# An attention block and a gated feed-forward layer on one core: the quadratic table made from products of projected rows instead of squared pair differences, in a new order, with the activation table asked for at the start

## The chip, the core and the metric

The kernel runs on one core of a Trainium2 chip. The metric is the device time of one execution in microseconds (us), smaller is better. An execution is profiled by the hardware; the profile gives each instruction's start and duration on each engine: PE (matmuls; PEld is its weight load), DVE (VectorE), ACT (ScalarE), POOL (GpSimd) and SP (which only issues transfers here). PSUM is the memory that PE writes and DVE and ACT read; it has 8 banks of 512 floats on each of 128 partitions.

## What is computed

`x` holds 4 batches of 12480 rows of 128 numbers, `inducing` 32 rows. All is float32.

```python
def mab(q, kv):
    s = scale * (q @ kv.transpose(0, 2, 1))
    s = s - s.max(-1, keepdims=True)
    a = np.exp(s)
    a /= a.sum(-1, keepdims=True) + 1e-09
    return a @ kv
h = mab(I, x)
return mab(x, h).astype(np.float32)
...
h = x @ w_in
relu6 = np.clip(h + 3.0, 0.0, 6.0)
g = h * relu6 / 6.0
return (g @ w_out).astype(np.float32)
```

So each batch first gives 32 rows H (every inducing row attends over the whole batch), then each of the 49920 rows attends over its batch's 32 rows H, and the result goes through a feed-forward layer with 2048 hidden units (`w_in` 128x2048, `w_out` 2048x128).

## The kernel before, in words

A row's second attention output is a weighted mean of the 32 rows H with weights a. Its 2048 hidden values are the same mean of the 32 projected rows G = H @ w_in. Where these stay within 3 of zero, the activation is (g*g + 3g)/6, so the final output is linear in the weights (32 rows through the whole layer, the table `BD`) plus a quadratic part that depends on the weights only through products a_m * a_n. The square of a mean is the mean of the squares less the sum over pairs of a_m * a_n * (G_m - G_n)^2, so the quadratic part needs one row of 128 outputs for each of 512 pairs (m, m + k): the **quadratic table** `Cq`, 4 blocks of 128 pairs by 128 outputs, bf16, made once for each batch.

Each batch of 12480 rows is cut in six groups of 2048 rows (16 tiles of 128) and one of 192 rows (2 tiles of 96). For each batch b there are three kinds of work.

Phase 1, by half groups: load `xr` (`op_X`, a transfer that POOL issues), cast to bf16 (`op_K`, on DVE, ACT or POOL), transpose 8 tiles on PE (`op_T`), copy out of PSUM (`op_Y`), scores against the inducing rows (`op_S`), exponential on ACT (`op_E`), weighted sum of rows on PE (`op_A`), running sums on DVE or POOL (`op_H`, `op_D`). Five buffers `xr` hold the loaded groups, and eight `xT` the transposed ones, since phase 2 uses them again.

The tables of batch b: `op_c1` to `op_c6` end in `HT` (H transposed, L503). From it `op_c9` makes the scores' weights, `op_G`, `op_cH`, `op_L`, `op_cM`, `op_cN` the linear table `BD` (L589). For the quadratic one `op_cA` and `op_cB` (L523, L526) form 512 columns of pair differences `dH` on DVE; sixteen `op_M` (L532) project them, one 128x512 matmul for each block of 128 hidden units; sixteen `op_N` (L540) square them on ACT into the twelve buffers `sq`; sixteen `op_P` (L598), four 128x128 matmuls each, sum `sq` against `w_out` into one bank, and `op_cP` (L608) scales this into `Cq`.

Phase 2, by groups: scores (`op_Z`), exponentials on ACT (`op_Zd` into `dk`, `op_Ze` into `e`), `op_W`, four transfers that SP issues and that repeat `dk` over partitions into `d`, the sum of weights (`op_R`), its logarithm on ACT (`op_Rl`, L655), normalised exponent (`op_Rz`), `op_Ra` (ACT), `op_Rh`, the spread to pairs (`op_B`, PE), pair weights (`op_F`, L703, ACT, two banks at once, into `TF`), times `d` on DVE (`op_U`, L712, into `TD`), then PE sums over the pairs (`op_q`, L747, 8 matmuls of 128x128 for each call, `TF` and `TD` against `Cq`) and over the linear table (`op_l`, L729), and `op_v` (L758, DVE or ACT) copies the result out for `op_O`, a transfer that SP issues.

The order of everything is written out by hand: `ORDER` is one list of 1583 tokens, and each token calls one `op_` function: `N.0.5.2.A` is `op_N` of batch 0, hidden block 5, PSUM bank 2, on ACT. Each engine runs its own instructions in the order of the list; waits come from the data. Phase 1 of the next batch, the tables and phase 2 of the batch before are interleaved in it. The list also says on which engine a cast or a copy runs (`V` DVE, `A` ACT, `P` POOL) and which bank is used. ACT evaluates exponentials and logarithms from a loaded function table; the program holds an `ACT_TABLE_LOAD` wherever the loaded table lacks the next function. `op_it` asks for a table that holds both; in `ORDER` of before this token comes late, in batch 1's tables. `op_w` are matmuls on a zero tile at the start that compute nothing.

Of the kernel before, what the change touches and what calls it, by code (L numbers as in the profile page):

```python
# [9 lines left out]
FP32 = mybir.dt.float32  # L10
FP32R = mybir.dt.float32r
# [12 lines left out]
i0.- X.0.0.8.16 i1.- X.0.0.0.8 i2.- w.2.6 X.0.6.0.2 w.2.0 i4.5 K.0.6.0.2.A w.2.3 w.2.0 w.2.2 i3.V T.0.6.0.2.4 i8.- w.2.3  # L24
w.2.7 i5.5.V X.0.1.0.16 i9.P X.0.2.0.16 ia.- K.0.0.8.16.V Y.0.6.0.2.4.A X.0.3.0.16 S.0.6.0.2.0 E.0.6.0.2.0 w.2.2
K.0.1.8.16.A K.0.0.0.8.V K.0.1.0.8.V A.0.6.0.2.0 c2.0.- T.0.0.0.8.1 T.0.0.8.16.2 Y.0.0.0.8.1.V T.0.1.0.8.5 T.0.1.8.16.4
S.0.0.0.8.1 Y.0.1.0.8.5.V Y.0.0.8.16.2.A Y.0.1.8.16.4.A K.0.2.0.8.V wi.- S.0.0.8.16.1 X.0.4.0.16 S.0.1.0.8.5 T.0.2.0.8.7
K.0.2.8.16.V S.0.1.8.16.5 E.0.0.0.16.1 A.0.0.0.8.1 T.0.2.8.16.3 D.0.0.V Y.0.2.0.8.7.V K.0.3.8.16.V A.0.0.8.16.1
E.0.1.0.16.5 Y.0.2.8.16.3.A A.0.1.0.8.5 S.0.2.0.8.7 T.0.3.8.16.4 K.0.3.0.8.V S.0.2.8.16.7 D.0.1.V i6.P Y.0.3.8.16.4.V
i7.P A.0.1.8.16.5 E.0.2.0.16.7 T.0.3.0.8.2 H.0.0.1 wh.0.V H.0.1.5 wh.1.A A.0.2.0.8.7 Y.0.3.0.8.2.A wh.3.A wh.2.A  # L30
X.0.5.0.16 wl.1.V A.0.2.8.16.7 D.0.2.V K.0.4.0.8.V X.1.0.0.16 wo.- wl.2.V S.0.3.0.8.2 S.0.3.8.16.2 H.0.2.7 T.0.4.0.8.6
E.0.3.0.16.2 A.0.3.0.8.2 Y.0.4.0.8.6.A X.1.1.0.16 K.0.4.8.16.P K.0.5.8.16.P T.0.4.8.16.1 A.0.3.8.16.2 X.1.2.0.16
S.0.4.0.8.4 K.0.5.0.8.A D.0.3.V Y.0.4.8.16.1.V S.0.4.8.16.4 E.0.4.0.16.4 K.1.0.0.8.P T.0.5.0.8.5 wl.3.V T.0.5.8.16.1
# [24 lines left out]
H.1.4.1 E.1.5.0.16.2 B.0.3.0.2.0 W.0.3 D.1.5.V Zd.0.4.4 q.0.1.2.1.5 q.0.1.3.1.7 A.1.5.0.8.4 K.2.1.0.8.P F.0.3.0.0.2
l.0.1.3.7 l.0.2.3.2 l.0.1.2.5 c1.1.- l.0.2.2.3 U.0.2.1 F.0.3.0.1.0 S.1.6.0.2.1 E.1.6.0.2.1 v.0.1.2.5.V A.1.5.8.16.4
v.0.1.3.7.A q.0.2.3.0.2 A.1.6.0.2.5 T.2.0.0.8.7 Ze.0.4.6 Ra.0.3 H.1.5.4 X.2.3.0.16 H.1.6.5 U.0.3.0 c2.1.- q.0.2.3.1.2  # L60
v.0.2.3.2.V q.0.2.2.0.3 O.0.1.0.16 q.0.2.2.1.3 B.0.3.1.0.4 X.2.4.0.16 Y.2.0.0.8.7.A W.0.4 c3.1.7 K.2.2.0.8.P
T.2.0.8.16.2 v.0.2.2.3.A c4.1.7 q.0.3.1.0.3 c5.1.7 l.0.3.1.3 F.0.3.1.0.0 F.0.3.1.1.4 c6.1.7 R.0.4.1 c7.1.A Z.0.5.0.7
Z.0.6.4.5 Y.2.0.8.16.2.V K.2.2.8.16.P Rl.0.4.1 S.2.0.0.8.2 Ze.0.5.7 c8.1.P cB.1.V q.0.3.1.1.3 Zd.0.5.0 S.2.0.8.16.2
T.2.1.8.16.1 cA.1.V M.1.2.0 Zd.0.6.4 Ze.0.6.5 Rz.0.4.6 l.0.3.0.4 R.0.5.6 c9.1.P E.2.0.0.16.2 Y.2.1.8.16.1.A T.2.1.0.8.2
q.0.3.0.0.4 G.1.3.1 Rl.0.5.6 U.0.3.1 Rh.0.4.V Y.2.1.0.8.2.V G.1.2.1 O.0.2.0.16 K.2.3.8.16.P G.1.1.1 G.1.0.1 Ra.0.4
v.0.3.1.3.A N.1.2.0.A Rz.0.5.7 W.0.5 q.0.3.0.1.4 v.0.3.0.4.A B.0.4.0.2.6 F.0.4.0.0.2 q.0.3.3.0.0 l.0.3.3.0 F.0.4.0.1.6
Rh.0.5.V l.0.4.1.4 cH.1.1 q.0.3.3.1.0 M.1.3.2 cJ.1.1 l.0.3.2.3 cI.1.1 v.0.3.3.0.V R.0.6.1 q.0.3.2.0.3 Rl.0.6.1
q.0.3.2.1.3 U.0.4.0 N.1.3.2.A K.2.3.0.8.P B.0.4.1.6.0 Ra.0.5 q.0.4.1.0.4 L.1.0.2 q.0.4.1.1.4 Rz.0.6.5 v.0.3.2.3.V
D.2.0.P q.0.4.0.0.3 M.1.0.5 l.0.4.0.3 Rh.0.6.V v.0.4.1.4.V F.0.4.1.0.6 F.0.4.1.1.0 N.1.0.5.A O.0.3.0.16 U.0.4.1
# [100 lines left out]

TG = 16
RT = 4
NX = 5
NXB = 2
NXT = 8
NSQ = 12
NTF = 3
NTD = 2
NNF = 2
NE = 2  # L180
ND = 2
NOS = 2
# [13 lines left out]
def kernel(  # L196
# [8 lines left out]
    nc = tc.nc  # L205
# [774 lines left out]
```

## Time and profile before

| | |
|---|---|
| median of 3 runs | 308.41 us (304.93, 308.41, 309.09) |
| the profiled execution's own time | 310.61 us |
| its span, first to last instruction | 308.8 us |
| mean granted PE clock | 0.962 of full speed |
| bytes moved | 66.69 MB |
| `HT` of the four batches ready (L503) | 35.7, 91.1, 165.5, 231.6 us |
| `Cq` of the four batches ready (L608) | 58.4, 134.1, 200.6, 264.1 us |

How to read it: "busy" is the time in which an engine had an instruction under way. Matmuls are pipelined, so PE's busy time includes their overlap, and one matmul's mean duration (about 220 ns for 128 columns) is far above the distance at which they follow each other; that distance is read from the chain of waits, where runs of matmuls stand with their count. The chain of waits is followed back from the last instruction: at each step to what released it, or to the instruction ahead of it on its engine.

### The profile page before, as it was taken

What the parts mean: (1) busy time and instruction counts of PE and PEld (TensorE: products, weight loads), DVE (VectorE), ACT (ScalarE), POOL (GpSimd) and SP (SyncE); (2) the same over time, 40 slices, a digit from 0 to 9 for tenths busy, and PEclk for the clock granted to TensorE, in tenths of its full rate; (3) what the DMA queues carried; (4) which work ended last, traced back from release to release, by engine and by line L of the source; (5) the groups of instructions that cost most, each with busy time, mean ns of one, the idle gap of its engine ahead of it and who ended that gap; (6) DMA issues with size and microseconds to landing.
All of it is one profiled execution on the core that took longest, in us unless ns stands there. A gap on an engine that the chain in (4) does not pass through costs nothing.

```text
span 308.8 us, 9738 instructions
## 1 busy us (share of the span) xinstructions
PE 275.8 (89%) x4105; PEld 216.8 (70%) x4105; DVE 218.5 (71%) x386; ACT 255.7 (83%) x416; POOL 65.7 (21%) x101
## 2 busy tenths in 40 slices
PE   6797878978986788999969999999999999999990
PEld 1587657766775565888848777787777777777780
DVE  4299996756766465575975766989788783799861
ACT  1377989998889799888955999789889999999980
POOL 8225533120345001144414001042302000000000
PEclk9597999999999599999997999999999999999998
DMA  6999984438698035676997351657547733777944
GB/s 154 419 348 409 346 248 153 138 70 330 212 326 293 2 142 179 184 231 182 338 385 240 138 183 42 197 156 240 180 104 270 248 141 69 222 231 244 326 163 155
DMA packets 23312, 66.69 MB, mean 216 GB/s; under 512 B 3648, under 2 KB 16736, under 8 KB 16992
## 3 DMA queue, kind: packets, MB, share of 16 engines
q1 hardware_dynamic: 18928, 38.36, 38.4%
q0 software_dynamic: 4336, 27.66, 25.8%
q8 instruction: 33, 0.54, 0.7%
q14 instruction: 15, 0.12, 0.1%
HBM read 27.67 MB, written 25.56 MB: 172 GB/s over the span
## 4 chain that ended last, share of the span: by engine, by line
PE 64%; ACT 13%; DVE 9%; DMA 7%; issue 3%; SPq 1%; POOL 0%; ACTq 0%; DVEq 0%; POOLq 0%
PE ps L747 25%; PE ps L729 7%; PE ps L426 6%; PE ps L453 5%; DMA d<-dk 5%; PE ps L693 5%; PE ps L598 4%; PE ps L532 3%; ACT TF L703 3%; PE ps L621 3%; DMA xl<-in_x_dram 2%; PE ps L437 2%; ACT L655 2%; PE ps L650 2%; DVE TD L712 2%
## 5 line engine op out<-in xcount | busy, mean ns | idle before, releaser
L703 ACT ACTIVATE TF<-ps 128x1024 bf16<-128x1024 f32 (+1 forms) x100 | 96.2, 1005 | 8.8 <-PE ps L693 7.3
L712 DVE TENSOR_TENSOR TD<-TF,d 128x2048 bf16<-128x2048 bf16 (+1 forms) x52 | 61.1, 1177 | 13.3 <-ACT TF L703 11.7
L747 PE MATMUL ps<-Cq,TD 128*128 128x128 bf16 (+1 forms) x784 | 59.9, 222 | 0.1
L747 PE MATMUL ps<-Cq,TF 128*128 128x128 bf16 (+1 forms) x784 | 59.3, 221 | 0.2
L758 DVE COPY os<-ps 128x512 f32<-128x512 f32 x62 | 42.2, 688 | 22.8 <-PE ps L747 17.8
L747 PEld LDWEIGHTS <-TF 128*128 128x128 bf16 (+1 forms) x784 | 46.6, 99 | 11.2 <-issue 9.1
L747 PEld LDWEIGHTS <-TD 128*128 128x128 bf16 (+1 forms) x784 | 47.4, 100 | 6.9 <-issue 4.6
L729 PE MATMUL ps<-BD,a 128*128 128x512 f32 (+1 forms) x100 | 39.2, 463 | 0.0
L420 POOL CAST xb<-xr 128x1024 bf16<-128x1024 f32 x24 | 28.1, 1180 | 51.7 <-PE ps L426 39.1
L540 ACT ACTIVATE sq<-ps 128x512 bf16<-128x512 f32 x64 | 35.2, 617 | 1.5 <-PE ps L532 1.4
L453 PE MATMUL ps<-xr,a 128*32 128x128 f32 x384 | 31.8, 229 | 3.1 <-ACT ln L655 2.2
L426 PE MATMUL ps<-ident_b,xb 128*128 128x128 bf16 x384 | 30.8, 232 | 3.0 <-DVE xb L420 1.8
L432 DVE COPY xT<-ps 128x1024 bf16<-128x1024 bf16 x32 | 21.8, 687 | 13.0 <-PE ps L426 11.9
L453 PEld LDWEIGHTS ps<-xr,a 128*32 128x32 f32 x384 | 25.4, 111 | 5.6 <-ACT ln L655 3.0
L426 PEld LDWEIGHTS <-xb 128*128 128x128 bf16 x384 | 24.9, 105 | 6.1 <-issue 3.7
L693 PE MATMUL ps<-z,pair 32*128 32x256 f16 (+1 forms) x400 | 21.3, 272 | 7.9 <-ACT os L758 2.4
L416 POOL DMA_DIRECT2D xr<-in_x_dram x25 | 15.7, 630 | 49.5 <-PE ps L453 26.2
L532 PE MATMUL ps<-dH,w_hi 128*128 128x512 bf16 x64 | 22.2, 384 | 3.3 <-ACT dk L631 1.8
L758 ACT COPY os<-ps 128x512 f32<-128x512 f32 x34 | 19.7, 590 | 4.9 <-PE ps L747 2.7
L660 DVE CUSTOM_DVE_ANT_0 zz<-ln,ps 128x512 f32<-128x512 f32 (+1 forms) x28 | 17.3, 619 | 9.0 <-ACT ln L655 8.8
L729 PEld LDWEIGHTS ps<-BD,a 128*128 128x128 f32 (+1 forms) x100 | 18.3, 196 | 4.9 <-ACT dk L631 2.0
L432 ACT COPY xT<-ps 128x1024 bf16<-128x1024 bf16 x16 | 16.2, 1015 | 5.1 <-PE ps L426 5.1
(145 smaller groups left out, 415.5 us busy)
## 6 DMA issues: line engine op xcount, KB each, us to landing
out_dram<-os SPq DMA_DIRECT2D x24, 1024.0 KB, 4.8
xr<-in_x_dram POOLq DMA_DIRECT2D x23, 1024.0 KB, 7.6
d<-dk SPq DMA_DIRECT2D x96, 128.0 KB, 3.2
xr<-in_x_dram POOLq DMA_DIRECT2D x2, 512.0 KB, 5.5
os<-in_moe_w_in_dram POOLq DMA_DIRECT2D x1, 1024.0 KB, 13.5
w_or<-in_moe_w_out_dram POOLq DMA_DIRECT2D x1, 1024.0 KB, 8.7
xl<-in_x_dram POOLq DMA_DIRECT2D x4, 96.0 KB, 5.9
out_dram<-osl SPq DMA_DIRECT2D x4, 96.0 KB, 4.3
```

The source lines that it names most:

```text
L420: copier(e)(at(xb, xbl, b, g)[:p, lo:hi, :], at(xr, xl, b, g)[:p, lo:hi, :].bitcast(FP32))
L426: nc.tensor.transpose(pt[:, (i - lo) * p : (i - lo + 1) * p], at(xb, xbl, b, g)[:p, i, :], ident_b[:p, :p])
L432: copier(e)(xT_of(b, g)[:, lo * p : hi * p], ps[:, k, :].bitcast(BF16)[:, : (hi - lo) * p])
L453: nc.tensor.matmul(ps[:M, k, :C], lhsT=at(a1, a1l, b, g)[:p, i * M : (i + 1) * M], rhs=at(xr, xl, b, g)[:p, i, :], start=(i == 0), stop=(i ...
L532: nc.tensor.matmul(ps[:, k, :], lhsT=w_hi[:, jb, :], rhs=dH[:, :, :, :, :].rearrange("p q k m i -> p (q k m i)"),)
L540: nc.scalar.activation(sq_of(b, jb)[:, :], ps[:, k, :], ACT.Square)
L693: nc.tensor.matmul(ps[:, pairs[j // 2] + j % 2, f * w : (f + 1) * w], lhsT=pair[rows, f].rearrange("p m i -> p (m i)"), rhs=fat(z_, b, g)[ ...
L703: nc.scalar.activation(hat(TF_, b, g, h)[:, 2 * q : 2 * q + 2, :w], ps[:, k : k + 2, :w], ACT.Exp, scale=-1.0)
L712: nc.vector.tensor_mul(split(hat(TD_, b, g, h)), split(hat(TF_, b, g, h)), d.unsqueeze(2).to_broadcast([P, J, 2, w]),)
L729: nc.tensor.matmul(ps[:p, k, : J * C], lhsT=fat(a_, b, g)[:rows, s * p : (s + 1) * p], rhs=BD_[b % 2][:rows, :J, :].rearrange("p j c -> p ...
L747: nc.tensor.matmul(ps[:p, k, j * C : (j + 1) * C], lhsT=t[:, j, f * w + s2 * p : f * w + (s2 + 1) * p], rhs=Cq_[b % 2][:, (1 + f) if u els ...
L758: copier(e)(at(os_, osl, b, g)[:p, s * J : (s + 1) * J, :], ps[:p, k, : J * C].rearrange("p (j c) -> p j c", c=C),)
```

## The change

The pair differences, their projection and their squares go. For a pair, -(G_m - G_n)^2 / 2 is G_m * G_n - G_m^2 / 2 - G_n^2 / 2, so the kernel now projects the 32 rows once and multiplies projected rows. In order: `op_cU` (three small DVE instructions) takes the mean of the rows H off and scales; `op_cg`, sixteen matmuls of 32 columns, projects; `op_gx` copies the 16x32 results out of PSUM as bf16 with 16 columns repeated at the end (two instructions); `op_g1` makes a copy shifted by one column; `op_gq` squares (512 columns). Sixteen `op_m` a batch on DVE multiply a row block `near` (`gb`, or the shifted `g1`) with `gb` at four offsets, 512 products at a time, bf16, into the three buffers `pr`. `op_P` is one matmul with `w_out` as the stationary operand and 512 columns of products, where it was four of 128 columns; its result stands with outputs on the partitions. `op_cs` sums the squares against `w_out` (sixteen matmuls of 32 columns), `op_cS` scales them by -1/2, `op_cT` adds the two ends of each pair, `op_cW` adds this to the products' sum, `op_ct` transposes four blocks on PE and `op_cP` copies them into `Cq`.

`ORDER` is written anew, 1566 tokens. `op_it` is now the third token. The first loads are the two halves of group 0 and groups 1 to 3; the small last group follows. `op_w` calls go from 8 to 24 (16 to 48 matmuls). Casts `op_K` on ACT go from 4 to 19, on DVE from 22 to 9, on POOL from 26 to 24; copies `op_v` on ACT from 35 to 59, on DVE from 65 to 41. The rings `xl`, `xbl`, `a1l`, `osl` of the small last group go from two buffers to one.

```diff
-i0.- X.0.0.8.16 i1.- X.0.0.0.8 i2.- w.2.6 X.0.6.0.2 w.2.0 i4.5 K.0.6.0.2.A w.2.3 w.2.0 w.2.2 i3.V T.0.6.0.2.4 i8.- w.2.3
+X.0.0.0.8 i2.- it.- X.0.0.8.16 w.2.7 X.0.1.0.16 i0.- w.2.3 w.2.4 w.2.0 X.0.2.0.16 i1.- i4.4 i3.V w.2.5 w.2.1 K.0.0.0.8.A
...
-NSQ = 12
+NPR = 3
...
+    root = 1.0 / math.sqrt(3.0 * 1024.0)
...
-        sq_ = ring("sq", NSQ, [P, 512], BF16)
+        pr_ = ring("pr", NPR, [P, 4, 4, P], BF16)
+        gb = sb.tile([P, FB, M + 16], BF16, name="gb")
+        g1 = sb.tile([P, FB, M], BF16, name="g1")
+        gq = sb.tile([P, FB, M], BF16, name="gq")
...
-        def op_cA(b, e):
-            veng(e).tensor_sub(dH[:, 0], shifted(HT, 0, 1, 0), shifted(HT, 2, 0, 4))
-
-        def op_cB(b, e):
-            veng(e).tensor_sub(dH[:, 1], shifted(HT, 1, -1, 0), shifted(HT, 4, 0, 4))
...
-        def op_M(b, jb, k):
-            nc.tensor.matmul(
-                ps[:, k, :],
-                lhsT=w_hi[:, jb, :],
-                rhs=dH[:, :, :, :, :].rearrange("p q k m i -> p (q k m i)"),
-            )
-
-        def op_N(b, jb, k, e):
+        def op_cU(b, e):
+            nc.vector.tensor_reduce(hm[:, :], HT[:, 0, :], axis=AX.X, op=ALU.add)
+            nc.vector.tensor_scalar_mul(hm[:, :], hm[:, :], -root / M)
+            nc.vector.tensor_scalar(
+                hc[:, :], HT[:, 0, :], root, hm[:, 0:1], op0=ALU.mult, op1=ALU.add
+            )
+
+        def op_cg(b, k):
+            for jb in range(FB):
+                nc.tensor.matmul(ps[:, k, jb * M : (jb + 1) * M], lhsT=w_hi[:, jb, :], rhs=hc[:, :])
...
+        def op_gx(b, k, e):
+            copier(e)(gb[:, :, :M], g_of(k))
+            copier(e)(gb[:, :, M:], g_of(k)[:, :, :16])
+
+        def op_gq(b, e):
             if e == "A":
-                nc.scalar.activation(sq_of(b, jb)[:, :], ps[:, k, :], ACT.Square)
+                nc.scalar.activation(gq[:, :, :], gb[:, :, :M], ACT.Square)
...
+        def op_g1(b, e):
+            copier(e)(g1[:, :, :], gb[:, :, 1 : M + 1])
+
+        def op_m(b, q, f):
+            rows = slice(4 * q, 4 * q + 4)
+            one, off = ((0, 2), (1, 2), (1, 4), (0, 4))[f]
+            near = (g1 if one else gb)[:, rows, :M]
+            a = gb[:, 4 * q, off : off + 1]
+            far = bass.AP(
+                tensor=a.tensor, offset=a.offset + off, ap=[a.ap[0], [M + 16, 4], [4, 4], [1, M]]
+            )
+            nc.vector.tensor_mul(
+                pr_[(4 * b + q) % NPR][:, :, f, :].rearrange("p a (i m) -> p a i m", m=M),
+                near.unsqueeze(2).to_broadcast([P, 4, 4, M]),
+                far,
+            )
...
         def op_P(b, jc, k):
             sums_of[b] += 1
+            nc.tensor.matmul(
+                ps[:, k, :],
+                lhsT=w_ob[:, jc, :],
+                rhs=pr_[(4 * b + jc // 4) % NPR][:, jc % 4, :, :].rearrange("p f n -> p (f n)"),
...
-                nc.tensor.matmul(
-                    ps[:, k, f * C : (f + 1) * C],
-                    lhsT=sq_of(b, jc)[:, f * P : (f + 1) * P],
-                    rhs=w_ob[:, jc, :],
...
+        def op_cs(b, k):
+            for jc in range(FB):
+                nc.tensor.matmul(
+                    ps[:, k, :M], lhsT=w_ob[:, jc, :], rhs=gq[:, jc, :], start=(jc == 0), stop=(jc == FB - 1)
+                )
...
+        def op_cW(b, k):
+            split = lambda t: t.rearrange("p (f i m) -> p f i m", f=4, m=M)
+            nc.vector.tensor_add(
+                CqT[:, :, :, :].rearrange("p f m i -> p f i m"), split(ps[:, k, :]), split(r6[:, :])
+            )
+            nc.vector.tensor_scalar_mul(CqT[:, 3, :, 3], CqT[:, 3, :, 3], 0.5)
+
+        def op_ct(b, k):
+            pt = ps[:, k, :].bitcast(BF16)
             for f in range(4):
...
+                nc.tensor.transpose(
+                    pt[:, f * C : (f + 1) * C],
+                    CqT[:, f, :, :].rearrange("p m i -> p (m i)"),
+                    ident_b[:, :],
                 )
```

Two places show how the instructions stand now. The first is ACT's queue just after batch 0's `HT`, where the tables are made and phase 2 begins. Before (`dk`, `e`, `ln` are phase 2, `sq` the squares, `a` phase 1's exponential):

```order
L636 ACTIVATE e_94<-ps 128x512
L655 ACT_TABLE_LOAD
L655 ACTIVATE ln_97<-ps 128x512
L540 ACTIVATE sq_115<-ps 128x512
L540 ACTIVATE sq_122<-ps 128x512
L540 ACTIVATE sq_117<-ps 128x512
L655 ACTIVATE ln_97<-ps 128x512
L540 ACTIVATE sq_121<-ps 128x512
L540 ACTIVATE sq_118<-ps 128x512
L445 ACT_TABLE_LOAD
L445 ACTIVATE a_90<-ps 128x512
```

And the change, in the same place (the lines have moved: L677 is `op_Ze`, L696 `op_Rl`, L438 `op_E`, L413 the casts of `op_K`, L402 `op_wb`, L540 `op_g1`):

```order
L677 ACTIVATE e_90<-ps 128x512
L425 COPY xT_77<-ps 128x1024
L413 CAST xb_75<-xr_72 128x1024
L696 ACTIVATE ln_94<-ps 128x512
L540 COPY g_115<-gb 128x512
L438 ACTIVATE a_87<-ps 128x512
L402 CAST w_ob<-w_or 128x512
L413 CAST xb_74<-xr_68 128x1024
L715 ACTIVATE a_92,s_all<-zz_95 128x512
```

The squares and the table loads are gone from ACT, and casts of phase 1, which wait for loads, stand among the exponentials. In the whole program ACT's rows hold 15 `ACT_TABLE_LOAD` before and one now, the first.

The second place is DVE's queue from batch 0's `HT` on. Before:

```order
L503 TENSOR_TENSOR HT<-ps,rD 128x64
L517 TENSOR_SCALAR HTq<-HT 128x64
L518 CAST HTs_131<-HTq 128x32
L520 TENSOR_TENSOR Wd_133<-HTq 128x32
L514 TENSOR_TENSOR HTl<-HT,HTb 128x32
L420 CAST xb_76<-xr_70 128x1024
L523 TENSOR_TENSOR dH<-HT 128x256
L526 TENSOR_TENSOR dH<-HT 128x256
L406 TENSOR_TENSOR w_lo<-os_112,w_hi 128x512
```

And the change, some rows further on (L530 and L531 are `op_gx`, L537 `op_gq`, L550 `op_m`, L569 to L577 the linear table):

```order
L518 TENSOR_SCALAR hc<-HT,hm 128x32
L457 COPY hacc_130<-ps 32x128
L530 CAST gb<-ps 128x16x32
L531 CAST gb<-ps 128x16x16
L537 TENSOR_TENSOR gq<-gb 128x512
L569 TENSOR_SCALAR r_139<-ps 128x512
L550 TENSOR_TENSOR pr_112<-gb 128x4x128
L572 SCALAR_TENSOR_TENSOR hs<-r_139,ps 128x512
L425 COPY xT_77<-ps 128x1024
L577 TENSOR_REDUCE g_all<-ps 128x1
L550 TENSOR_TENSOR pr_113<-gb 128x4x128
```

DVE had two instructions of the quadratic table behind `HT`; now its products stand among copies and phase 2's instructions, sixteen a batch.

More of the change, by code (lines that the diff above doesn't have):

```diff
@@ L29 @@
[L29 to L33, printed above, removed]
@@ L293 @@
         pair = sb.tile([P, 2, M, 4], FP16, name="pair")
-        fac = sb.tile([P, 4], FP32, name="fac")
-        i_of = sb.tile([P, 1], I32, name="i_of")
         z_all = sb.tile([P, B * NGR], FP32, name="z_all")
@@ new lines, in op_cs, with op_cS, op_cT @@
+        def op_cs(b, k):
[3 more added lines that the diff above has]
+                )
+        def op_cS(b, k):
+            nc.vector.tensor_scalar_mul(S_sb[:, :M], ps[:, k, :M], -0.5)
+            nc.vector.tensor_scalar_mul(S_sb[:, M:], ps[:, k, :16], -0.5)
+        def op_cT(b, e):
+            o = r6[:, :].rearrange("p (f i m) -> p f i m", f=4, m=M)
+            a = S_sb[:, 0:1]
+            for one, fs, off, step in ((0, o[:, 0::3], 2, 2), (1, o[:, 1:3], 2, 2)):
+                near = bass.AP(tensor=a.tensor, offset=a.offset + one, ap=[a.ap[0], [0, 2], [0, 4], [1, M]])
+                far = bass.AP(tensor=a.tensor, offset=a.offset + off, ap=[a.ap[0], [step, 2], [4, 4], [1, M]])
+                veng(e).tensor_tensor(fs, near, far, op=ALU.add)
```

314 lines of the change are left out of this document (154 added, 160 removed).

## The prediction

> **What bounds the kernel now.** I read the busy times first, then the same by stretches, then the chain of waits.
>
> ```profile
> PE 275.8 (89%) x4105; PEld 216.8 (70%) x4105; DVE 218.5 (71%) x386; ACT 255.7 (83%) x416; POOL 65.7 (21%) x101
> ```
>
> PE and ACT are both nearly full, so the question is which of them, and where. I cut the span at batch 0's `HT` (35.7 us) and at batch 1's `Cq` (134.1 us).
>
> ```profile
> core 0: us, PE busy (x) PEld busy (x) DVE busy (x) ACT busy (x) POOL busy (x), PEclk, DMA share, GB/s
> 0.00:35.70 35.70, 27.20 (x338) 21.03 (x339) 24.12 (x48) 19.44 (x26) 16.49 (x43) 0.86 0.94 332
> 35.70:134.10 98.40, 84.37 (x1268) 65.84 (x1269) 63.89 (x111) 89.89 (x142) 24.29 (x29) 0.97 0.61 201
> 134.10:303.50 169.40, 164.20 (x2509) 129.95 (x2501) 130.53 (x229) 146.35 (x249) 24.94 (x30) 0.99 0.63 204
> ```
>
> The start is full of transfers (DMA share 0.94). In the middle stretch ACT is busy for 89.89 of 98.4 us, 91%, and PE for 86%. In the last, PE is busy for 164.20 of 169.4, 97%, and ACT for 86%. So ACT sets the middle and PE the rest. The chain agrees:
>
> ```profile
> PE 64%; ACT 13%; DVE 9%; DMA 7%; issue 3%; SPq 1%; POOL 0%; ACTq 0%; DVEq 0%; POOLq 0%
> ```
>
> Pieces of it, in order of time:
>
> ```profile
> 3.10 6.15 DMA xl<-in_x_dram
> 10.08 1.71 PE ps L353 x4
> ...
> 37.16 1.34 DVE dH L523
> ...
> 45.04 1.28 ACT L445
> 46.34 0.60 ACT a L445
> ...
> 86.73 8.02 DMA d<-dk
> ...
> 153.53 7.16 DMA d<-dk
> ...
> 168.80 0.59 PE ps L549 x24
> ...
> 183.81 0.65 PE ps L532 x3
> ...
> 262.58 1.45 PE ps L598 x24
> ...
> 298.35 2.25 PE ps L747 x40
> ```
>
> The rows without an output (45.04) are table loads standing on the chain itself. The last four give PE's real distances: 25 ns a matmul of 32 columns (L549), 217 ns for 512 (L532), 56 to 60 ns for 128 (L747, L598).
>
> **The change, part by part.** These groups carry it:
>
> ```profile
> L758 DVE COPY os<-ps 128x512 f32<-128x512 f32 x62 | 42.2, 688 | 22.8 <-PE ps L747 17.8 <-PE ps L729 4.9
> ...
> L540 ACT ACTIVATE sq<-ps 128x512 bf16<-128x512 f32 x64 | 35.2, 617 | 1.5 <-PE ps L532 1.4
> ...
> L758 ACT COPY os<-ps 128x512 f32<-128x512 f32 x34 | 19.7, 590 | 4.9 <-PE ps L747 2.7 <-PE ps L729 2.1
> ...
> L420 DVE CAST xb<-xr 128x1024 bf16<-128x1024 f32 x22 | 15.3, 708 | 4.6 <-DMA xr<-in_x_dram 4.6
> ...
> L655 ACT ACT_TABLE_LOAD x7 | 9.0, 1283 | 2.0 <-PE ps L650 1.9
> ...
> L608 DVE TENSOR_TENSOR Cq<-ps,fac 128x512 bf16<-128x512 f32 x4 | 2.8, 692 | 1.3 <-PE ps L598 1.2
> ...
> L445 ACT ACT_TABLE_LOAD x2 | 2.6, 1283 | 0.0
> L674 ACT ACT_TABLE_LOAD x2 | 2.6, 1283 | 0.0
> ...
> L420 ACT CAST xb<-xr 128x1024 bf16<-128x1024 f32 x2 | 2.1, 1041 | 0.0
> ...
> L420 ACT ACT_TABLE_LOAD x1 | 1.3, 1283 | 0.7 <-PEq L964 0.7
> L703 ACT ACT_TABLE_LOAD x1 | 1.3, 1283 | 0.0
> L636 ACT ACT_TABLE_LOAD x1 | 1.3, 1283 | 0.0
> L334 ACT ACT_TABLE_LOAD x1 | 1.3, 1283 | 0.0
> ```
>
> *ACT.* 15 table loads become one: 14 x 1.283 = 18.0 us less, 13 of them after the start. The 64 squares go: 35.2 less. 24 more copies out at 0.59 are 14.2 more, 14 more full casts at 1.04 are 14.6 more. Of the rest, about eight casts and squares added at 0.59 and less, four removed at 0.59 and two at 1.04, leave +1. Sum 255.7 - 18.0 - 35.2 + 14.2 + 14.6 + 1 = 232 us.
>
> A rule of the Trainium skill sets the first term otherwise. "ScalarE: Activation LUTs", section "What ACT_TABLE_LOAD costs", gives about 1283 ns for the load and about 1380 ns of draining behind it, 2.66 us a switch; by it the term would be an estimated 37 instead of 18. The trace has the load at 45.04 to 46.32 and the next activation at 46.34, so it shows the load and no drain, and the sum keeps 18.0.
>
> *PE.* Removed: 64 matmuls of 512 columns, 13.9 us, and 256 of 128 at 56 ns, 14.3. Added: 64 of 512, 13.9; 128 of 32, 3.2; 16 transposes, 0.9. Net 10.2 us less, 2.55 a batch. Almost all of it comes from projecting 32 rows instead of 512 differences; one wide matmul (217) for four narrow ones (224) is worth nothing. The 32 added zero matmuls cost up to 0.43 each (L353), 13.7 us, but most stand in the first 9 us, where PE waits for the first load (6.15 us on the chain). Without that cover the start would be some 6 us longer.
>
> *DVE.* Removed: 13 casts at 0.708 (9.2), 24 copies at 0.688 (16.5), four times 0.69 at `Cq`, and `dH`. Added: the 64 products, whose price no row shows. The nearest rows, kept apart by shape:
>
> ```profile
> L712 DVE TENSOR_TENSOR TD<-TF,d 128x2048 bf16<-128x2048 bf16 x48 | 59.3, 1237 | 11.8 <-ACT TF L703 10.4 <-ACT xT L432 1.4
> L712 DVE TENSOR_TENSOR TD<-TF,d 128x384 bf16<-128x384 bf16 x4 | 1.8, 451 | 1.5 <-ACT TF L703 1.4
> L473 DVE TENSOR_TENSOR dacc<-dacc,a 128x512 f32<-128x512 f32 x13 | 11.9, 917 | 0.1
> L523 DVE TENSOR_TENSOR dH<-HT x4: 589/614/1424, 37.1 to 232.6; 128x256 bf16<-128x256 f32 x4
> ```
>
> L712 also multiplies bf16 with one operand repeated over a middle dimension, and its runs are contiguous, as `op_m`'s are. A quarter of its wide form is 0.31, its two forms interpolated at 512 columns give 0.51: the bounds if it packs alike. Float32 at 512 columns took 0.917; that is the upper bound. I take 0.45, nearest to L712. Small additions (`gx`, `cW`, `cP` and three on the side, 512 columns out of PSUM at 0.69, and some 25 little ones at about 0.2) are 5.5 + 5, and four more copies and casts 2.5. `dH` takes off eight at its median of 0.614, 4.9. So 218.5 - 9.2 - 16.5 - 2.8 - 4.9 + 13 + 28.8 = 227 us.
>
> *Order and waits.* Fifteen more casts stand on ACT and wait for loads there; exponentials and PSUM copies queue behind them, and PE behind those. On DVE these waits came to 4.6 us (row L420), so that is the price if loads are late. The `near` and `far` products are ahead of PE's `op_P` in time by construction of the list; if they come late, PE's `op_q` of the group before waits behind `op_P`, as it now does behind the squares. `w_out`'s load is put behind three loads of batch 1; phase 1 of batch 1 and the products hide it, since only `op_cs` and `op_P` need it; late, it would hold these and `Cq` for as long as it is late. The single buffers of the small group bind only one batch later.
>
> **The sum.** By PE: batch 0 and 1 fall in the middle stretch, 2 and 3 in the last, 5.1 us less in each. With ACT relieved, I give the middle stretch PE's fill of the last, 0.97: (84.37 - 5.1) / 0.97 = 81.7. The last gives 169.4 - 5.1 / 0.97 = 164.1. The start I leave at 35.7 (first work earlier, DVE has 1 to 2 us more there), and 308.8 - 303.5 = 5.3 remains behind. Sum 286.8. By ACT: 232 - 19.4 = 213 after the start, at the last stretch's 0.864, is 246.5; with start and tail 287.5. DVE: 227 - 24.1 = 203 at 0.864 is 235, so it isn't first. Both give a span of 287, 22 less. The profiled execution took 310.61 with span 308.8; the median of the runs shown is 308.41, so I put the median at the span: **287 us**. Filled as well as ACT now is in the middle (0.913), the 213 us of ACT would give 35.7 + 233 + 5.3 = 274; filled at 0.82 because three engines now bind at once, 301. The likeliest case itself runs from 276 to 299.
>
> **Rivals.**
>
> *Transfers take the freed time.* All 66.69 MB remain, in less time, and the chain already waits 8.02 and 7.16 us for `d`. Two more such waits give 287 + 15 = 302. For it: the start's share of 0.94, and those two pieces. Against: share 0.61 and 0.63 elsewhere.
>
> *The products don't pack.* At 0.917 they cost 58.7; DVE after the start is 203 + 30 = 233, at 0.864 269.7, with start and tail 310.7: no change. For it: four-dimensional operands, offset columns. Against: L712 and the shifted copy `g1`.
>
> *Slower: products locked out by POOL.* The first `dH` took 1.34 on the chain, beside POOL's casts:
>
> ```profile
> 36.52 2.89 POOL L420 CAST xb<-xr 128x1024 bf16<-128x1024 f32 x2 [0.46 <-DVE Wd L520]
> ```
>
> At its shortest `dH` takes 0.59 (row L523), so it stretches where they overlap. If two thirds of the products met a POOL instruction and took `dH`'s longest, 1.42, the mean would be 1.10, DVE 203 - 28.8 + 70.4 = 245 after the start, 283 at 0.864, and the time 324. It decides from a mean of 0.90 on (then DVE has 231 us of work in the 267.8 that lie between start and tail now, at 0.864). Against: POOL is busy for 21%. The Trainium skill names it, "SBUF — State Buffer", section "Who interferes with whom": a DVE instruction with two SBUF inputs and a GpSimd instruction that reads SBUF exclude each other; the stretched `dH` agrees.
>
> *The drain is real.* Then ACT stands still behind every load for as long again, 14 x 1.28 = 18 more comes back, and the time is 269. By the page above it is an estimated 19. The activation that starts at 46.34 speaks against it.
>
> **Chances.** Forecast 0.76; transfers 0.12, half of it under the bound; products that don't pack 0.05; slower 0.04; drain 0.03. A measurement of this kernel tells about 2% from no change, so faster means under 302.2: 0.76 + 0.06 + 0.03 and a little of the mixed cases, 0.87; within 2% 0.09; slower 0.04. Range 275 to 300.
>
> **What would show it.** One table load on ACT, its busy time near 232; products (L550) near 0.45 us; ACT no longer above 90% and PE near 97% over the stretch between batch 0's `HT` and the last store; no table load on the chain. I'd be wrong if the products are above 0.6, if `d<-dk` or `xr` pieces on the chain grow past 25 us, or if PE stands idle behind ACT's casts.

## The result and the profile after

The changed kernel took 286.22 us (median of 4 runs, 284.75 to 288.22), the kernel before 308.75 on the same chip (4 runs, 304.93 to 309.30): 0.930 of the time, 95% interval 0.919 to 0.940. The forecast was 287, between 275 and 300. The profiled execution took 284.75 us, with a span of 282.8. Where a kernel's comparison leaves single disturbed executions out (one of 594.21 us at the first kernel with fewer zero matmuls, one of 286.23 at the kernel with the small load kept, one of 322.92 of the kernel before beside it), its interval is over the others.

First the busy times, then the granted clock in 40 slices, and the shares of the chain of waits by engine:

```profile
PE 262.7 (93%) x4011; PEld 202.3 (72%) x4025; DVE 224.1 (79%) x438; ACT 231.1 (82%) x382; POOL 71.1 (25%) x107
...
PEclk9999999999999999999999989999999999999996
...
PE 52%; DVE 4%; DMA 3%; ACT 3%; issue 1%; SPq 1%; ACTq 0%; DVEq 0%
```

ACT fell by 24.6 us and PE by 13.1; DVE rose by 5.6. On the chain, which is followed back only to 96.6 us here, ACT has 3%. The stretch in which ACT had been the bound, from batch 0's `HT` to batch 1's `Cq`, and then from that `HT` up to the last batch's and from there to the end:

```profile
33.80:100.10 66.30, 60.47 (x977) 46.39 (x979) 59.61 (x125) 55.72 (x93) 24.20 (x29) 1.00 0.74 246
```

```profile
33.80:203.70 169.90, 159.93 (x2563) 126.18 (x2568) 139.98 (x273) 141.88 (x242) 53.39 (x60) 0.99 0.68 225
203.70:282.80 79.10, 71.80 (x1052) 53.63 (x1055) 60.60 (x121) 66.44 (x113) 3.15 (x6) 0.97 0.63 205
```

The columns are those of the prediction's table by stretches. In the first row ACT is busy for 84% (it was 91%), PE for 91%. Batch 1's `Cq` is ready 34 us earlier than before, but less of the other work lies ahead of it in the new list, so the later cuts say more: the last `HT` comes at 203.7 instead of 231.6, 27.9 us earlier, and the rest takes 79.1 instead of 77.2. All of the gain lies ahead of the last `HT`.

The granted clock differs too. Behind the first `HT` it falls to half in two spells before, and in one after, leaving the end aside:

```profile
101.20:108.00 6.80, 6.03 (x43) 4.35 (x43) 3.02 (x5) 4.93 (x9) 0.00 (x0) 0.50 0.01 2
162.60:166.00 3.40, 3.40 (x28) 3.04 (x26) 2.34 (x3) 1.77 (x3) 1.93 (x2) 0.50 0.85 345
```

```profile
162.00:165.40 3.40, 3.07 (x36) 2.29 (x36) 1.60 (x5) 2.55 (x8) 1.04 (x1) 0.50 0.28 116
```

By an estimate from these lengths, half of 10.2 less 3.4, some 3 of the 27.9 us are clock. Most of the gain isn't: executions of the kernel before with a mean clock of 0.990 and 0.982 (beside the second series of experiments) took 304.26 and 305.60 us, the changed kernel 284.75 at 0.986.

The groups that carry the sum, by line, engine and shape:

```profile
L799 ACT COPY os<-ps 128x512 f32<-128x512 f32 x58 | 33.8, 599 | 5.1 <-PE ps L788 4.2 <-PE ps L770 0.4 <-ACT TF L744 0.2
...
L550 DVE TENSOR_TENSOR pr<-gb 128x512 bf16<-128x512 bf16 x32 | 18.2, 581 | 0.0
...
L413 ACT CAST xb<-xr 128x1024 bf16<-128x1024 f32 x16 | 16.7, 1052 | 6.2 <-DMA xr<-in_x_dram 6.2
...
L550 DVE TENSOR_TENSOR pr<-g,gb 128x512 bf16<-128x512 bf16 x32 | 14.6, 469 | 0.0
...
L636 DVE TENSOR_TENSOR CqT<-ps,r 128x512 bf16<-128x512 f32 x4 | 5.2, 1309 | 2.6 <-PE ps L608 2.6
...
L335 ACT ACT_TABLE_LOAD x1 | 1.3, 1283 | 0.7 <-PEq L1005 0.7
```

The products kept DVE busy for 0.51 us each (32.8 us for 64), against 0.45 forecast. The new cost that was priced wrongly is `CqT`, 1.31 us where 0.69 was taken; there are only four. (In `op_m`, `far` starts at `a.offset` in the kernel, not at `a.offset + off`: `a` already begins at column `off`.)

### The profile page after: what moved, and what is told of

Read it like the earlier page. It is cut to its first block, busy times and chain, and to the rows that moved or that the text cites. A ratio compares the mean times of both kernels' runs of the same rounds, so it can differ in the third digit from the quotient of the medians.

```text
span 282.8 us, 9597 instructions
## 1 busy us (share of the span) xinstructions
PE 262.7 (93%) x4011; PEld 202.3 (72%) x4025; DVE 224.1 (79%) x438; ACT 231.1 (82%) x382; POOL 71.1 (25%) x107
## 4 chain that ended last, share of the span: by engine, by line
PE 52%; DVE 4%; DMA 3%; ACT 3%; issue 1%; SPq 1%; ACTq 0%; DVEq 0%
PE ps L788 24%; PE ps L770 7%; PE ps L734 4%; PE ps L446 3%; DMA d<-dk 3%; PE ps L662 3%; PE ps L419 2%; PE ps L608 2%; ACT TF L744 2%; PE ps L691 2%; DVE CqT L636 1%; DVE TD L753 1%; PE ps L430 1%; PE ps L560 1%; PE ps L583 1%
## 5 line engine op out<-in xcount | busy, mean ns | idle before, releaser
L753 DVE TENSOR_TENSOR TD<-TF,d 128x2048 bf16<-128x2048 bf16 (+1 forms) x52 | 62.4, 1200 | 6.3 <-PE ps L788 3.3
L788 PE MATMUL ps<-Cq,TD 128*128 128x128 bf16 (+1 forms) x784 | 58.4, 219 | 0.3 <-DVE TD L753 0.3
L788 PEld LDWEIGHTS <-TF 128*128 128x128 bf16 (+1 forms) x784 | 45.5, 98 | 9.4 <-issue 7.9
L413 POOL CAST xb<-xr 128x1024 bf16<-128x1024 f32 x23 | 27.7, 1210 | 52.5 <-PE ps L419 29.8
L799 ACT COPY os<-ps 128x512 f32<-128x512 f32 x58 | 33.8, 599 | 5.1 <-PE ps L788 4.2
L799 DVE COPY os<-ps 128x512 f32<-128x512 f32 x38 | 25.9, 687 | 11.1 <-PE ps L770 4.5
L419 PE MATMUL ps<-ident_b,xb 128*128 128x128 bf16 x384 | 28.5, 221 | 5.5 <-ACT ln L696 3.2
L446 PE MATMUL ps<-xr,a 128*32 128x128 f32 x384 | 30.9, 227 | 0.5 <-DVE CqT L636 0.5
L419 PEld LDWEIGHTS <-xb 128*128 128x128 bf16 x384 | 23.1, 99 | 9.6 <-issue 7.1
L446 PEld LDWEIGHTS ps<-xr,a 128*32 128x32 f32 x384 | 24.6, 109 | 3.9 <-issue 1.3
L409 POOL DMA_DIRECT2D xr<-in_x_dram x25 | 13.9, 557 | 41.1 <-PE ps L446 18.8
L438 ACT ACTIVATE a<-ps 128x512 fp32r<-128x512 f32 x24 | 14.4, 600 | 9.1 <-PE ps L430 6.7
L413 ACT CAST xb<-xr 128x1024 bf16<-128x1024 f32 x16 | 16.7, 1052 | 6.2 <-DMA xr<-in_x_dram 6.2
L672 ACT ACTIVATE dk<-ps 128x512 bf16<-128x512 f32 (+1 forms) x28 | 15.1, 552 | 5.1 <-DMA d<-dk 5.0
```

What stands on the lines that cost most here:

```text
L413: copier(e)(at(xb, xbl, b, g)[:p, lo:hi, :], at(xr, xl, b, g)[:p, lo:hi, :].bitcast(FP32))
L419: nc.tensor.transpose(pt[:, (i - lo) * p : (i - lo + 1) * p], at(xb, xbl, b, g)[:p, i, :], ident_b[:p, :p])
L446: nc.tensor.matmul(ps[:M, k, :C], lhsT=at(a1, a1l, b, g)[:p, i * M : (i + 1) * M], rhs=at(xr, xl, b, g)[:p, i, :], start=(i == 0), stop=(i ...
L672: nc.scalar.activation(fat(dk_, b, g)[:rows, :w], ps[:rows, k, :w], ACT.Exp)
L753: nc.vector.tensor_mul(split(hat(TD_, b, g, h)), split(hat(TF_, b, g, h)), d.unsqueeze(2).to_broadcast([P, J, 2, w]),)
L788: nc.tensor.matmul(ps[:p, k, j * C : (j + 1) * C], lhsT=t[:, j, f * w + s2 * p : f * w + (s2 + 1) * p], rhs=Cq_[b % 2][:, (1 + f) if u els ...
```

## Experiments

Each ran on one chip with its own runs of the kernel before, whose median is named. Theory throughout: table loads and squares made ACT the bound of the middle, PE is the bound of the rest, and the new order is no more than what keeps both fed.

**The table request alone, in the kernel before.**

```diff
-i0.- X.0.0.8.16 i1.- X.0.0.0.8 i2.- w.2.6
+it.- i0.- X.0.0.8.16 i1.- X.0.0.0.8 i2.- w.2.6
...
-D.2.1.P it.- N.1.7.2.A
+D.2.1.P N.1.7.2.A
```

> The kernel before, with nothing changed but the place of the request for the activation table, which goes first. Theory (ACT bound the middle stretch, 14 loads of 1.283 us stood in it): ACT's 89.89 us of work there fall by 18.0 to 72, PE's 84.37 at its fill of 0.97 become the bound, the 98.4 us of the stretch shrink to 87, the time falls by 11, to 297 (294 to 300), and ACT stays at 238 busy in all. Rival (the loads stood beside other waits, and the gain comes from the new products and order): within 3 us of the kernel before. Rival (a drain behind each load): 18 or more less, 290.

Measured: 296.23 us (291.82 to 301.28) beside 307.38 (303.65 to 314.88), 11.2 less in the medians and 11.8 in the shortest runs. Its four runs lie 9.5 us apart, so the size is known to a few us only; the span of the profiled execution, 292.5, is 16.3 below that of the kernel before. Its stretch from batch 0's `HT` to batch 1's `Cq`:

```profile
36.00:120.70 84.70, 80.52 (x1268) 64.13 (x1272) 62.09 (x110) 72.52 (x128) 25.44 (x29) 0.98 0.71 234
```

The same 1268 matmuls now take 84.7 instead of 98.4 us; ACT has 72.5 us of work in it, and PE is busy for 95%. So ACT was the bound there and PE took over, as the theory says. ACT's whole busy time, 237.8, is 17.9 less, which is 14 loads of 1.283. A drain would stand as idle time and not as busy time; in the trace of the kernel before ACT's next instruction starts 0.01 to 0.08 us behind the end of each of these 14 loads, and 13 of them start 0.02 us behind the instruction ahead, so none is seen.

**The table request late, in the changed kernel**, at its old place.

```diff
-X.0.0.0.8 i2.- it.- X.0.0.8.16
+X.0.0.0.8 i2.- X.0.0.8.16
...
-D.2.1.P R.0.6.6
+D.2.1.P it.- R.0.6.6
```

> The changed kernel, with the request for the table back at its old place in the program (behind the sum D of batch 2, group 1), 14 loads on ACT. Theory: ACT's 81.82 us of work in the stretch from the first HT to 130 us grow by up to 17 to about 98, that is more than the stretch holds, so it grows by some 10 us and the time goes to 296 (292 to 301). Rival (PE is the bound there by now and covers them): 286 to 289.

Measured: 299.35 us (295.76 to 301.82), 0.981 of the kernel before (0.968 to 0.993). The same stretch:

```profile
33.80:110.60 76.80, 63.69 (x982) 48.09 (x979) 58.77 (x125) 71.17 (x105) 24.50 (x29) 0.98 0.65 215
```

ACT rises from 55.72 to 71.17 us and is busy for 93%; the stretch is 10.5 us longer, which is nearly all of the 11.1 by which the span grew. PE does not cover them. By the medians the request is worth 11 us alone and 13 on top of the rest; by the spans of the profiled executions it is 16 and 11.

**The new tables in the old order.** In the old list each square's place takes a product, the first and second projection's places take `op_cg` and `op_cs`, the wide `op_P` follow as their products are made, and every cast and copy stays on its engine. The first loads and the 16 zero matmuls are those of the old list, the buffers those of the changed kernel (single ones for the small last group). A piece of batch 0, with the request late (the first of two kernels; the second has it first):

```diff
-cA.0.V cB.0.V Ze.0.0.6 M.0.0.2 R.0.0.1 Zd.0.0.5 wl.0.V M.0.7.5 Ze.0.1.7
+cU.0.- Ze.0.0.6 cg.0.2 R.0.0.1 Zd.0.0.5 wl.0.V Ze.0.1.7
...
-N.0.0.2.A Y.1.1.0.8.3.V M.0.2.1 M.0.3.0 M.0.6.2 K.1.2.8.16.P
+gx.0.2.A g1.0.A gq.0.A m.0.0.0 Y.1.1.0.8.3.V cs.0.1 K.1.2.8.16.P
```

> The new products and wide matmuls written into the old order: casts and copies on the engines of before, each square's place taken by a product, the table request late (15 loads). ACT falls by 35 to 220, PE by 10 to 265, DVE rises by the products (33) and the small additions to about 255. Theory (the work moved from DVE to ACT is needed, DVE being the next bound): DVE's 231 us after the start at 0.9 give 257, with start and tail 298 (292 to 306), so two thirds of the gain is missing. Rival (the gain comes from the squares and PE's matmuls and needs no new order): 286 to 291.

> As the one before, with the table request first (one load). ACT 202, PE 265, DVE 255. Theory (DVE is then the bound over the whole, whatever ACT does): 292 to 300, within 5 us of the one with the late request, since ACT has slack in both. Rival (the new order adds nothing, table and squares and matmuls are all of it): 284 to 289.

Measured: 322.76 us with the late request (320.05 to 325.52; 1.052 of before, 1.040 to 1.064) and 315.11 with the early one (311.84 to 319.54; 1.026, 1.013 to 1.039). Both expectations missed, and the rival more so: the new algebra in the old list is slower than the squares were. The busy times of the second:

```profile
PE 271.9 (86%) x3993; PEld 207.9 (65%) x3993; DVE 243.9 (77%) x473; ACT 215.4 (68%) x354; POOL 64.2 (20%) x100
```

No engine is near full over the span, which speaks against DVE's amount of work, which the theory held responsible. Whether DVE's time is what is lacking was asked next.

**The same with the new engines**: in that list 14 casts and 24 copies go from DVE to ACT, places unchanged, and `gq` to DVE. For example:

```diff
-gx.0.2.A g1.0.A gq.0.A
+gx.0.2.A g1.0.A gq.0.V
```

> The new products in the old order with the table request first, and now as many casts (14) and PSUM copies (24) moved from DVE to ACT, batch by batch, as the changed kernel has on ACT; the rows keep their places. DVE falls from 244 to about 222, ACT rises from 215 to 242. Theory (what the old order lacked is DVE's time): 286 to 294, nearly all of the 28 us that separate it from the changed kernel. Rival (the places in the list matter as much as the engines, since every engine works its list in order): 300 to 312.

Measured: 330.27 us (328.95 to 331.96) beside 308.96: 1.069 (1.063 to 1.075). The work is now spread as in the changed kernel, and the time is longer still, 13 us (by the ratios) to 15 (by the medians) over the kernel with the casts on DVE, and beyond the rival's range. From the first `HT` to the last, and from there on:

```profile
41.60:247.80 206.20, 179.41 (x2643) 137.43 (x2641) 143.32 (x283) 150.86 (x252) 44.98 (x55) 0.95 0.57 183
247.80:328.40 80.60, 69.65 (x1020) 52.38 (x1019) 58.67 (x120) 61.65 (x107) 1.12 (x4) 0.97 0.61 201
```

The last batch takes 80.6 us, close to the changed kernel's 79.1. The first `HT` comes at 41.6 instead of 33.8, and the stretch between, where the next batch's phase 1 and tables are interleaved with phase 2, takes 206.2 us instead of 169.9: PE is busy for 87% where the changed kernel has 94, DVE and ACT for 70 and 73%. The longest of PE's waits in it are these; the rest are many and short:

```profile
PE ps L608 <- DVE pr L550: 5.1, 4, 2.0
PE ps L430 <- DVE xT L425: 2.9, 1, 2.9
PE ps L734 <- ACT TF L744: 2.6, 4, 1.6
```

The mean clock in it is 0.95 and not 0.99, so that by an estimate from the two rows some 9 of the 36.3 us more are clock (0.05 x 206.2 less 0.01 x 169.9). The casts on ACT cost time ahead of it: PE's waits for them all lie before the first `HT`, which came at 37.9 with the casts on DVE.

```profile
PE ps L419 <- ACT xb L413: 6.6, 4, 2.3
PE ps L419 <- ACT xbl L413: 3.0, 1, 3.0
```

So DVE's time isn't what the old list lacked: in it the new algebra doesn't pay, whichever engine does the casts and copies. What the new list is worth by itself isn't shown, since no kernel had it with the old squares. Whether another way of writing the new tables into the old list would do better wasn't tried, and which of its places cost most stays open.

**More and fewer products.** First each product is computed twice into the same place:

```diff
-            nc.vector.tensor_mul(
+            for _ in range(2):
+                nc.vector.tensor_mul(
```

> The changed kernel with every product on DVE computed twice into the same place, 64 more instructions, and nothing else changed. At the 0.51 us that they took in the mean DVE rises by 33 to 257. Theory (DVE is not first but close: 117 of 147.5 us in the last stretch): a part of it shows, 8 to 18 us, 294 to 304. Rival (DVE already sets the end): 33 us more, 319. Rival (products lie in DVE's slack): under 4 us, 290 at most. In it the mean of a product shows whether the surplus over 0.41 us comes from POOL: the second of two beside no POOL work stays at 0.41.

Measured: 312.43 us (310.76 to 313.70), 1.019 of 306.57 (1.010 to 1.029): 26 us more than the changed kernel, for 30.9 us of work on DVE (255.0 busy). A product took 0.42 us in the median there too, so the second one of each pair costs what the first does. PE now waits at `op_P` for products, which it did not in the changed kernel:

```profile
PE ps L609 <- DVE pr L551: 10.2, 5, 3.7
```

That is above the theory's 294 to 304 and nearer to the rival, by which DVE sets the end. The other direction tells more. Here the two middle shifts are left out, 32 products; zeros written once on POOL (5.3 us at the start) stand in their place, so two quarters of the table lack their products:

```diff
+            if f in (1, 2):
+                return
             rows = slice(4 * q, 4 * q + 4)
...
+            for t in pr_:
+                nc.gpsimd.memset(t[:, :, :, :], 0.0)
```

> The changed kernel without 32 of its 64 products (those of the two middle shifts; zeros stand in their place, so two quarters of the quadratic table lack their products). DVE falls by 15 to 209, ACT and PE keep their work. Doubling the products had cost 26 us for 31 of DVE work. Theory (PE is at 97% outside the middle, DVE follows closely behind): 1 to 5 us less, 281 to 285. Rival (DVE sets the time as it did with doubled products): 12 us less, 274.

Measured: 287.81 us (287.22 to 289.93), 0.933 of 308.96 (0.927 to 0.938), no faster than the changed kernel. DVE fell by 9.5 us, to 214.6, less than the 15 of the expectation. So the rival's 12 us are not there and DVE doesn't set the changed kernel's time, yet nearly each microsecond added to it shows: the products stand where PE's `op_P` comes soon behind them, and the list has little slack for their being late. The theory's 1 to 5 us did not show either, but they aren't excluded: behind the zeros POOL issues its next load at 14.21 us instead of 8.52, the first `HT` comes at 35.0 instead of 33.8, and the profiled execution has 6.8 us at half clock (from 46.1 on) that the changed kernel's lacks.

**Narrow sums**: each wide `op_P` as four matmuls of 128 columns with the same weights.

```diff
-                ps[:, k, :],
+                ps[:, k, f * C : (f + 1) * C],
                 lhsT=w_ob[:, jc, :],
-                rhs=pr_[(4 * b + jc // 4) % NPR][:, jc % 4, :, :].rearrange("p f n -> p (f n)"),
+                rhs=pr_[(4 * b + jc // 4) % NPR][:, jc % 4, f, :],
```

> The changed kernel with each wide matmul of 512 columns that sums the products taken apart into four of 128 columns with the same weights, 192 matmuls more. Theory (four narrow ones at 56 ns cost what a wide one costs at 217): 285 to 288, no difference that shows, PE busy within 2 us. Rival (the wide matmul is a good part of the gain, by fewer weight loads and issues): 64 times 0.1 or more, 6 to 12 us slower.

Measured: 284.94 us (283.56 to 285.49), 0.930 of 306.57 (0.922 to 0.938), as the changed kernel. PE is busy 2.1 us more, the weight loads 9.1 more (PEld 211.4), and both are hidden. A wide matmul is worth nothing here, as forecast.

**The zero matmuls.** First those behind the first transpose are left out (24 of 48 stay), then all but 8:

```diff
-T.0.0.0.8.2 w.2.6 T.0.0.8.16.7 Y.0.0.0.8.2.V w.2.5 w.2.6
+T.0.0.0.8.2 T.0.0.8.16.7 Y.0.0.0.8.2.V
```

> The changed kernel without those of its zero matmuls that stand behind the first transpose of the first batch; the rest stay. Theory (they stand in PE's waits for the first loads): within 2 us of the changed kernel, 284 to 288. Rival (what lies behind the first transpose costs PE its time, 0.4 us each): 3 to 8 us faster. Rival (they keep TensorE's granted clock up while loads are waited for): slower by 2 us or more, with a lower granted clock in the first 34 us.

> The changed kernel with 8 of its 48 zero matmuls, those ahead of everything else; the others, up to the first sums, are left out. Theory of the prediction (they only fill time in which PE waits for the first loads): 283 to 287, granted clock 1.00 from 9 to 35 us as in the changed kernel. Rival (they keep the granted clock up through the first loads, which the kernel before ran at 0.80): the clock falls to about 0.8 there, the first HT comes 1 to 3 us later than 33.8, and the time is 287 to 291.

Measured: 289.30 us for the first (286.73 to 290.22; 0.946 of 306.57, 0.936 to 0.956), above the 284 to 288 expected, and 284.83 for the second (283.02 to 285.61; 0.920 of 308.96, 0.915 to 0.925). With the fewest the kernel is no slower, so the first one's 3 us aren't theirs; its runs had granted clocks of 0.96 to 0.97, the second's 0.97 to 1.00, and why is open (its profiled execution has two spells at half clock, 6.8 us from 45.5 and 3.4 from 100.1, that the changed kernel's lacks). The start of the second, then of the kernel before cut at the same time:

```profile
0.00:33.80 33.80, 26.07 (x363) 20.75 (x364) 23.68 (x44) 22.56 (x28) 14.55 (x42) 1.00 0.97 359
```

```profile
0.00:33.80 33.80, 25.74 (x321) 19.89 (x322) 22.56 (x43) 17.54 (x23) 15.28 (x41) 0.85 0.93 330
```

PE is busy for about as long in both, with 363 matmuls at 1.00 and 321 at 0.85 of the clock, and the first `HT` comes at 33.9 with 8 zero matmuls and at 33.8 with 48. The 40 left out neither cost time nor hold the clock up.

**The wait for `d`.** One transfer piece stands out on the chain after: `d` of batch 1's sixth group, issued just behind a 1 MB store and beside 1 MB of `x`.

```profile
152.85 8.60 DMA d<-dk
161.56 0.60 ACT dk L672
162.15 0.14 ACT ln L696
```

```diff
-R.1.5.3 O.1.2.0.16 l.1.3.1.7 W.1.5 cs.2.2 X.3.5.0.16
-m.2.0.3 Ra.1.4 Rl.1.5.3 X.3.6.0.2
+R.1.5.3 l.1.3.1.7 W.1.5 cs.2.2 m.2.0.3 Ra.1.4 Rl.1.5.3
...
-Rl.1.6.7 U.1.4.0 T.3.2.0.8.5
+Rl.1.6.7 U.1.4.0 O.1.2.0.16 X.3.5.0.16 X.3.6.0.2 T.3.2.0.8.5
```

> The changed kernel with the store of batch 1's third group and the last loads of x of batch 3 issued behind the copies of dk to d of batch 1's sixth group, instead of ahead of them. Theory (that d waits 8.60 us because both of these share the DMA engines with it at 153 us): the wait falls to about 4 us and the time by 3 to 5 us, 281 to 284. Rival (the wait is hidden by other work, or moves to the next transfer): within 1.5 us of the changed kernel.

Measured: 287.48 us (285.69 to 287.87), 0.937 of 306.57 (0.928 to 0.945): no gain, as the rival had it. The wait for `d` is gone, and another stands there, for the small load that had been moved too; a cast on ACT waits for it and PE behind that cast's engine, 3.4 us as it had been 3.2:

```profile
160.01 5.70 DMA xl<-in_x_dram
165.71 0.02 issue
165.74 0.03 ACT xbl L413
```

So the small load (`X.3.6.0.2`) was put ahead of `W.1.5`, and only the two large transfers behind it. Against the changed kernel:

```diff
-R.1.5.3 O.1.2.0.16 l.1.3.1.7 W.1.5 cs.2.2 X.3.5.0.16
-m.2.0.3 Ra.1.4 Rl.1.5.3 X.3.6.0.2
+R.1.5.3 l.1.3.1.7 X.3.6.0.2 W.1.5 cs.2.2 m.2.0.3 Ra.1.4 Rl.1.5.3
...
-Rl.1.6.7 U.1.4.0 T.3.2.0.8.5
+Rl.1.6.7 U.1.4.0 O.1.2.0.16 X.3.5.0.16 T.3.2.0.8.5
```

> As the kernel with the store and the loads behind the copies of dk to d, but with the small load of x (96 KB, for which a cast on ACT waited 3.4 us there) left ahead of them. Theory (the collision at 150 us costs 3 to 4 us, and it only went to that load): no wait above 2 us on PE between 100 and 172 us, 281 to 284. Rival (PE's time is given back by the next wait or by the clock): 284 to 288.

Measured: 282.51 us (281.68 to 286.23), 0.913 of 308.96 (0.908 to 0.918). The longest waits of PE between 100 and 172 us are these:

```profile
PE ps L608 <- DVE pr L550: 0.9, 1, 0.9
PE ps L430 <- issue: 0.7, 1, 0.7
```

The wait is gone and nothing took its place, and the spell at half clock that the changed kernel has at 162.0, at the end of this wait, is missing too. The last `HT` comes at 201.1 instead of 203.7, 2.6 us earlier, and the rest takes the same 79.2. The interval lies just under the changed kernel's (0.919 to 0.940), which ran on another chip. On the same chip the kernel with 8 zero matmuls, otherwise the changed one, took 284.83 us, 2.3 us or 0.8% more. A gain of about 1% is likely and fits the 2.6 us; it is too small to be called shown.

## Why the prediction was right, point by point

*Bounds.* ACT in the middle: shown from both sides by moving the table request alone (84.7 for 98.4 us) and by taking it back (10.5 us). PE elsewhere is argued: it was busy for 94 to 97%, and less work on DVE brought no gain that shows; no run took work from PE alone.

*ACT's sum.* 232 forecast, 231.1 measured; 1.052 and 0.599 us for casts and copies instead of 1.04 and 0.59. The load without a drain holds: 17.9 us less for 14 loads, all of which stood after the start (the prediction put 13 there), and no idle time behind them. The Trainium skill's 1380 ns of draining ("ScalarE: Activation LUTs", "What ACT_TABLE_LOAD costs") would have made this about 37 by estimate; it doesn't say on which side of the load the draining stands, and the trace of the kernel before shows none on either.

*PE's sum.* 10.2 less of issue time was forecast, and the early request leaves about as much to the rest: 296.2 to 286.2 us, on two chips. That doesn't show the term, since the rest is also the new list, the engines and the start. The wide matmul is worth nothing, shown. The fill after the start was 95% (231.73 of 249.0 less the 5.3 behind the last store) and not 97; the work itself was less (231.7, where 84.37 + 164.20 - 10.2 = 238.4 was reckoned with), in part since more of it had gone into the start (355 matmuls besides the zero ones in the kernel with 8 of these, against 322 before) and in part since less of it ran at half clock. The two nearly cancel, which is luck: 243.7 us for 245.8. As for 2.55 us in each batch, the last one shows none of it: PE is busy there for 71.80 us, before for 70.27.

*DVE's sum.* 227 forecast, 224.1 measured, with the products and `CqT` above their prices and the rest below. The products pack (0.41 and 0.42 us in the medians of the two shapes); the higher mean comes from a few. What was called the slower rival's mechanism is seen, at a small price. DVE's and POOL's rows in time:

```profile
47.83 0.41 DVE L550 TENSOR_TENSOR pr<-gb 128x512 bf16<-128x512 bf16 x1
48.16 0.27 DVE L459 TENSOR_TENSOR hacc<-hacc,ps 32x128 f32<-32x128 f32 x1
48.36 1.77 DVE L550 TENSOR_TENSOR pr<-g,gb 128x512 bf16<-128x512 bf16 x1
50.06 1.49 DVE L550 TENSOR_TENSOR pr<-gb 128x512 bf16<-128x512 bf16 x1
```

```profile
48.56 2.72 POOL L466 TENSOR_TENSOR dacc<-dacc,a 128x512 f32<-128x512 f32 x2
51.21 0.57 POOL L409 DMA_DIRECT2D xr<-in_x_dram  x1
```

The two products beside POOL's additions take 1.77 and 1.49 us, the one ahead of them 0.41. The 40 products with no POOL instruction beside them took 0.40 to 0.42 us, and each one above 0.45 overlaps with one. Over all 64 the surplus is 32 x (0.581 + 0.469) - 64 x 0.41, 7.4 us. The Trainium skill says that a DVE instruction with two SBUF inputs and a GpSimd instruction that reads SBUF exclude each other ("SBUF — State Buffer", "Who interferes with whom"); this pair of rows agrees. The mean stayed far under the 0.90 from which it was to decide.

*Order and waits.* Here the prediction was incomplete. It gave the new list no term, only "if they come late" as a risk. The three kernels in the old list show that with the same algebra a list can take 23 us (both with the late request) to 44 us more than the new one, a lower clock included. The sum by busy times and a fill came out right because the changed list reaches that fill; nothing in the sum could have told that. The fill of 97% was an assumption, not a result of the work moved. The clock had no term either.

*The start.* Left at 35.7, measured 33.8; the granted clock there was 1.00 and not 0.86. The cover for the zero matmuls was not needed, since 8 do as well as 48. Their price of 0.43 us was read at 10.08 us, where the clock was 0.50 (from 9.0 to 15.8 us); in the changed kernel the first eight take 3.59 us, but the sixteen from 4.96 us on 3.64, 0.23 each.

*Transfers.* Waits for `d` stayed at 8.60 us in one place and cost some 3 us; the rival's 15 did not come.

## What to carry to other kernels

Take the cheapest part of a change (here one token) as a kernel of its own: it gave half of the gain or more. Where every engine works a fixed list, a sum of busy times over a fill is a forecast for a list that fits the new durations, and not for the old list with new instructions in it. An engine whose work can be cut without a gain that shows can still cost nearly one for one when work is added, if others wait close behind it.

## What the runs showed of the hardware

The granted clock over the first 33.8 us was 0.85 in the kernel before and 1.00 in the changed one, with 48 zero matmuls and with 8. In the kernel before, PE stands idle for 3.87 us ahead of its first transpose at 9.74 us; with 8 zero matmuls the changed kernel has gaps of 1.51 and 0.76 us and its first transposes at 6.54. In the profiled executions of these two, leaving the last microseconds aside, the clock is 1.00 but for spells of 3.4 or 6.8 us at 0.50, and each of these begins at the end of a stop of PE or shortly behind it: in the kernel before at 9.0, 26.1, 101.2 and 162.6 us, with stops from 5.9 to 9.7, 23.9 to 25.8, 99.6 to 102.0 and 159.5 to 161.5; in the changed kernel at 162.0, with a stop from 159.1 to 162.3. Not each stop brings one. A stop of 1.90 us at 42.0 in the kernel with the store moved was followed by 6.8 us at half clock from 44.9 on (0.94 in the mean from 35 to 100 us), and one of 1.65 us at the same place in the changed kernel by none (1.00), though both run the same instructions up to there. That stops of PE lower the clock would fit, and wasn't tried by itself. An addition of 128x512 that reads PSUM and writes bf16 at every fourth element (`CqT`) took 1.31 us, a plain copy of that size 0.69.
